# Weight pieces of a fused attention and mixture-of-experts kernel: other staging tiles, deeper staging, a third kind of conversion buffer

## The chip, the core and the metric

The kernel runs on one core of one Trainium2 chip. The core's engines are TensorE (PE in the rows, PEld its weight loads), VectorE (DVE), ScalarE (ACT), GpSimd (POOL) and SyncE (SP), which here does nothing but issue DMAs. The metric is the device time of one execution in microseconds, as a median of runs.

## The reference

Three layers follow one another, for 4 batches, 8 heads, 576 positions and 64 values a head:

```python
scores = scale * np.matmul(q, k.transpose(0, 1, 3, 2))
kth = np.partition(scores, -32, axis=-1)[..., -32:-31]
attn = softmax(np.where(scores >= kth, scores, -1e9))       # the 32 largest of each row
x = (attn @ v), heads side by side: 2304 rows x 512
x = (sigmoid(x @ w_gate) * (x @ w_val)) @ w_out              # 512 -> 1536 -> 512
# then 8 experts, top 2 by noisy logits: relu(x @ w1[e]) @ w2[e], weighted, added
```

The weights w_gate (512 x 1536), w_val (512 x 1536) and w_out (1536 x 512) are read by the kernel as 64-bit words and turned into pairs of 16-bit floats, a high part and the rest, on the chip.

## The kernel before

**Order of the work.** All operations are written down with an engine, an assumed duration, a priority (a lower number goes first), the operations they depend on, and the buffers that they take, each by a tag with a capacity (CAPS, line 174). A planner then goes through assumed time and, on each engine, lets the ready operation of lowest priority number go whose buffers are free. So the order of instructions on each engine is fixed when the kernel is built; on the chip each engine works through its own list, waiting on semaphores where an operand or a buffer isn't ready. Operations that take the same tag on the same engine go in the order in which they were written down.

**Attention** goes in units: one pair of heads (hp, 0 to 3) and one block of 128 query rows, a tile for each head (the last 64 rows of a batch make smaller units). For each, PE makes scores, ACT copies them out (line 355), DVE finds the top values of eight stretches and of these (lines 364 to 373), POOL and ACT prepare the ranking (390, 399, 405), DVE finds the 32nd value and masks the exponents (412, 427), PE transposes them (456, 476) and multiplies by the values (497). The exponents lie in buffers of tag e (4), the ranked copies in y (4). A unit has the priority 10 i, where i counts the tiles before it: 0, 20, 40 and so on. The keys and queries of a head pair of batch 0 are loaded through two st buffers (line 215) with priorities −10, −5, 5 and 15 for the four pairs; the values of the batch (line 259) with −5.

**Gate, value and output layer.** Four units of one row block make a chunk of 128 rows; the first two row blocks of batch 0 are chunks 0 and 1, the next two together are chunk 2 with 256 rows and eight units. A chunk takes a buffer xch (2 of them) when its first unit is opened, ahead of that unit's transposes, and holds it until its last gate and value product. For a chunk, PE goes through 12 hidden blocks of 128 columns (line 537; ACT's tanh, line 544, stands at each), needing weight tile WA[f // 2] for block f, then through the output weights WO (line 576). This work has the unit's priority plus 1000, so it fills what attention leaves of PE.

**The weights.** There are 36 pieces of 512 KB: 24 of w_gate and w_val, four for each of six tiles WA[0] to WA[5] (`wa_ops`), and 12 of w_out, four for each of three tiles WO[0] to WO[2] (`wo_ops`). Their priorities are 0, 4, ..., 20 for WA and 24, 28, 32 for WO. One piece is made by `weight_piece` (lines 265 to 291): SP loads it into an st buffer (274); ACT turns its low words into integers in place (282); DVE puts the bits of the high words into a conversion buffer, two instructions (280, 281); POOL adds the low part (285), after which the st buffer is free; ACT writes the high 16-bit part (286); the rest is made either by DVE (288, one piece in four) or by ACT and POOL (290, 291), after which the conversion buffer is free. The conversion buffers are of tag x2 (2 of them) for two pieces in three and of tag y for the third. There are three st buffers, and the loads of keys, queries and weights take them in the order written down: the four head pairs of batch 0, then the pieces.

The tiles WA and WO come from one pool of nine buffers (`wpool`), which the experts' weights use again later. The tag x2 also serves the layer's result (585) and the first fill of a table (929). Small inputs of the router are loaded by `load_small` (940 to 943), ten DMAs with priority 26.

Of the kernel before, what the change touches and what calls it, by code (L numbers as in the profile page):

```python
# [11 lines left out]
FT = mybir.dt.float32  # L12
FH = mybir.dt.float16
BF = mybir.dt.bfloat16
I32 = mybir.dt.int32
U32 = mybir.dt.uint32
AF = mybir.ActivationFunctionType
# [3 lines left out]
B, H, S, D = 4, 8, 576, 64  # L21
N, DM, F1 = B * S, H * D, 1536
# [104 lines left out]
def attention_moe_kernel(ctx: ExitStack, tc: tile.TileContext, qT, kT, v, w_gate, w_val, w_out,  # L127
# [38 lines left out]
    for b in range(B):  # L166
# [5 lines left out]
    nst = const.tile([128, N // 128, E], FT, name="nst")  # L172

    CAPS = dict(st=3, w=0, tb=4, khl=5, v=5, sS=6, sg=2, m=5, y=4, e=4, pt=2, xch=2, xrem=1, th=2, g=10, x2=2,
                ps=1, tp=3, mm=3, px=3)

    def layers(fast):
        outer = ExitStack()
# [83 lines left out]

        npiece = [0]

        def weight_piece(src, k, f, hi, lo, scale, prio):
            tag = ("x2", "y", "x2")[npiece[0] % 3]
            npiece[0] += 1
            hs, hw = plan.tile("st"), plan.tile(tag)
            t = Unit()

            def load():
                st = stage.tile([128, 2 * S], FT, name="st", bufs=CAPS["st"]).bitcast(I32)[:, :1024]
                t.st = st.rearrange("p (k f c) -> p k f c", k=k, c=2)
                nc.sync.dma_start(t.st.rearrange("p k f c -> p k (f c)"), src.rearrange("(k p) f -> p k f", p=128))
            a = op("SP", 2.6, prio, load, alloc=[hs], lat=3.0)

            def bits():
                t.y = tile_of(tag, [128, SW if tag == "y" else DM], FT)[:, :512].rearrange("p (k f) -> p k f", k=k)
                t.i = t.y.bitcast(I32)
                V.tensor_scalar(t.i, t.st[:, :, :, 1], 3, 0x3FFFFFFF, op0=OP.logical_shift_left, op1=OP.bitwise_and)  # L280
                V.scalar_tensor_tensor(t.i, t.st[:, :, :, 1], -0x40000000, t.i, op0=OP.bitwise_and, op1=OP.bitwise_or)
            r = op("ACT", 0.53, prio, lambda: A.activation(t.st[:, :, :, 0], t.st.bitcast(U32)[:, :, :, 0], AF.Copy,
                                                           scale=2.0 ** -29), [a], use=[hs])
            b = op("DVE", 1.1, prio, bits, [a], alloc=[hw], use=[hs])
            b = op("POOL", 1.2, prio, lambda: G.tensor_tensor(t.i, t.i, t.st[:, :, :, 0], op=OP.add), [r, b], use=[hs, hw])
            c = op("ACT", 0.55, prio, lambda: A.activation(hi(), t.y, AF.Copy, scale=scale), [b], use=[hw])
            if npiece[0] % LOD[0] < LOD[1]:
                return op("DVE", 0.65, prio, lambda: V.scalar_tensor_tensor(lo(), t.y, scale, hi(), op0=OP.mult, op1=OP.subtract),
                          [c], use=[hw])
            d = op("ACT", 0.55, prio, lambda: A.activation(t.y, t.y, AF.Copy, scale=scale), [c], use=[hw])  # L290
            return op("POOL", 1.2, prio, lambda: G.tensor_tensor(lo(), t.y, hi(), op=OP.subtract), [d], use=[hw])  # L291
# [3 lines left out]
        def wa_ops(g, prio):  # L295
# [9 lines left out]
                        sc, prio))  # L305
            WA.append(w)

        def wo_ops(j, prio):
            w = Unit()
            w.h = plan.tile("w")  # L310
            w.t = wpool.tile([128, 4096], FH, name="w").rearrange("p (c k f) -> p c k f", c=2, k=4)
            w.done = [weight_piece(w_out[(4 * j + i) * 128:(4 * j + i + 1) * 128], 1, 512,
                                   lambda i=i: w.t[:, 0, i:i + 1], lambda i=i: w.t[:, 1, i:i + 1], SO, prio)
                      for i in range(4)]
            WO.append(w)


        ranks, scores = [], []
# [623 lines left out]
            for a, src in ((0, wg), (1, wn)):  # L942
                nc.sync.dma_start(wr[:, :, 8 * a:8 * a + 8], src.rearrange("(k p) e -> p k e", p=128))
        if fast:
            op("SP", 5.0, 26, load_small)

        def init_out(prio):
            q, hz = Unit(), plan.tile("x2")
# [109 lines left out]
```

## Time and profile before

| | us |
|---|---|
| median of 3 runs | 1373.16 |
| lowest, highest | 1369.38, 1375.27 |
| the profiled execution | 1367.3 |
| its span, first to last instruction | 1365.5 |
| PE, DVE, ACT, POOL busy in it | 1212.1, 897.1, 814.6, 724.6 |
| mean granted clock of PE | 0.952 |

The profile is of one execution. It gives each instruction of each engine with its start and end, the line of the kernel, and what ended the idle time before it. "Busy" is the union of an engine's instructions, waits on semaphores left out. The granted clock is a share of 2.4 GHz; it has two levels, 1.2 and 2.4 GHz, and a figure between is a mixture over time.

### The profile page before, as it was taken

What the parts mean: (1) busy time and instruction counts of PE and PEld (TensorE: products, weight loads), DVE (VectorE), ACT (ScalarE), POOL (GpSimd) and SP (SyncE); (2) the same over time, 40 slices, a digit from 0 to 9 for tenths busy, and PEclk for the clock granted to TensorE, in tenths of its full rate; (3) what the DMA queues carried; (4) which work ended last, traced back from release to release, by engine and by line L of the source; (5) the groups of instructions that cost most, each with busy time, mean ns of one, the idle gap of its engine ahead of it and who ended that gap; (6) DMA issues with size and microseconds to landing.
All of it is one profiled execution on the core that took longest, in us unless ns stands there. A gap on an engine that the chain in (4) does not pass through costs nothing. (4 is left out here: it accounts for less than half of the span.)

```text
span 1365.5 us, 29938 instructions
## 1 busy us (share of the span) xinstructions
PE 1212.1 (89%) x10829; PEld 899.2 (66%) x10830; DVE 897.1 (66%) x3656; ACT 814.6 (60%) x1818; POOL 724.6 (53%) x985
## 2 busy tenths in 40 slices
PE   2447479699999999999999999899999999999997
PEld 1226356487686868776877778776766666666674
DVE  5998998888999789988778772463233524334221
ACT  4767678777887778777757754562243424424221
POOL 2889998788677586776566562333221222212221
PEclk9667699799999999999999999999999999999999
DMA  8434331362004300051000021264234545443321
GB/s 190 126 107 126 99 124 52 96 174 106 17 14 102 112 2 17 13 132 43 17 2 17 9 94 48 86 208 80 50 94 120 135 81 163 103 107 90 53 45 21
DMA packets 63376, 111.82 MB, mean 82 GB/s; under 512 B 14449, under 2 KB 23793, under 8 KB 63218
## 3 DMA queue, kind: packets, MB, share of 16 engines
q1 hardware_dynamic: 53106, 89.84, 22.3%
q0 software_dynamic: 10112, 19.97, 8.1%
q8 instruction: 87, 1.43, 0.5%
q14 instruction: 71, 0.58, 0.1%
HBM read 79.58 MB, written 20.63 MB: 73 GB/s over the span
## 5 line engine op out<-in xcount | busy, mean ns | idle before, releaser
L537 PEld LDWEIGHTS <-w 128*128 128x128 f16 x3456 | 277.3, 100 | 45.1 <-issue 18.0
L537 PE MATMUL mm<-xch,w 128*128 128x256 f16 (+1 forms) x2880 | 284.1, 256 | 15.0 <-ACT xch L507 5.7
L405 POOL TENSOR_TENSOR y<-sS,sg 128x576 f32<-128x576 f32 x144 | 196.9, 1367 | 9.1
L808 PE MATMUL mm<-xch,w 128*128 128x256 f16 (+1 forms) x2016 | 193.0, 256 | 0.0
L808 PEld LDWEIGHTS <-w 128*128 128x128 f16 x2016 | 170.8, 98 | 23.9
L816 DVE SCALAR_TENSOR_TENSOR g<-mm,g 128x256 f16<-128x256 f32 (+1 forms) x192 | 72.6, 380 | 163.4 <-ACT g L813 162.4
L364 DVE MAX8 cand<-sS 128x8 f32<-128x72 f32 x1152 | 166.7, 217 | 16.4 <-ACT sS L355 16.2
L576 PE MATMUL mm<-w,g 128*128 128x512 f16 x648 | 156.2, 385 | 4.4 <-POOL w L291 2.2
L834 PEld LDWEIGHTS <-g 128*128 128x128 f16 x960 | 93.3, 98 | 98.8
L779 POOL DMA_INDIRECT v<-xd,ids x40 | 42.1, 1052 | 207.6 <-DVE ws L769 192.2
L813 ACT ACTIVATE g<-mm 128x256 f16<-128x256 f32 (+1 forms) x192 | 66.8, 348 | 140.4 <-PE mm L808 134.5
L427 DVE SCALAR_TENSOR_TENSOR e<-sS,good,e 128x576 f32<-128x576 f32 x144 | 139.3, 987 | 1.8 <-ACT e L382 0.7
L554 POOL TENSOR_TENSOR g<-th,g 128x128 f16<-128x128 f32 (+1 forms) x144 | 98.3, 688 | 71.8 <-ACT g L551 70.6
L347 PE MATMUL ps<-khl,qs 128*128 128x288 f16 x512 | 94.6, 313 | 44.9 <-ACT sS L355 26.6
L399 ACT ACTIVATE sg<-sS,m 128x576 bf16<-128x576 f32 x144 | 110.5, 769 | 33.5 <-POOL m L390 33.0
L846 POOL DMA_INDIRECT out<-e,ids x40 | 63.8, 1594 | 123.2 <-ACT e L843 84.8
L412 DVE MAX8 good<-y 128x8 f32<-128x584 f32 x144 | 109.9, 763 | 20.0 <-POOL y L405 15.4
L497 PE MATMUL tp<-pt,v 128*64 128x128 f32 (+3 forms) x1600 | 116.7, 284 | 7.1 <-ACT pt L463 2.8
L834 PE MATMUL tp<-w,g 128*128 128x512 f16 x504 | 114.8, 379 | 0.0
L497 PEld LDWEIGHTS tp<-pt,v 128*64 128x64 f32 (+1 forms) x1600 | 84.6, 142 | 41.0 <-issue 21.1
L456 PE MATMUL tp<-ident,e 128*128 128x128 f32 x576 | 90.0, 291 | 24.4 <-DVE e L427 23.0
L576 PEld LDWEIGHTS <-g 128*128 128x128 f16 x648 | 63.2, 99 | 69.3 <-issue 9.4
(163 smaller groups left out, 2139.3 us busy)
## 6 DMA issues: line engine op xcount, KB each, us to landing
st<-w SPq DMA_DIRECT2D x64, 512.0 KB
khl<-st SPq DMA_DIRECT2D x48, 144.0 KB
st<-w_gate SPq DMA_DIRECT2D x12, 512.0 KB
st<-w_val SPq DMA_DIRECT2D x12, 512.0 KB
st<-w_out SPq DMA_DIRECT2D x12, 512.0 KB
st<-k_t SPq DMA_DIRECT2D x20, 288.0 KB
st<-q_t SPq DMA_DIRECT2D x20, 288.0 KB
xd<-x SPq DMA_DIRECT2D x18, 256.0 KB
```

Of the source, the lines that this page charges most:

```text
L347: P.matmul(o, kqr.qs[:, t, u.q0:u.q0 + 128], kqr.khl[:, c, t, ks], start=c == 0, stop=c == 1)
L364: V.max(T[t].cand[:, 8 * c:8 * c + 8], T[t].s[:, 72 * c:72 * c + 72])
L399: A.activation(T[t].sg, T[t].s, AF.Sign, scale=-CUT[0], bias=T[t].m[:, 25:26], accum_out=T[t].m[:, 26:27])
L405: G.tensor_tensor(T[t].y[:, :S], T[t].s, T[t].sg, op=OP.mult)
L412: V.max(good[:, TILES - 1 - u.i - t:TILES + 7 - u.i - t], T[t].y)
L427: return lambda: V.scalar_tensor_tensor(T[t].e, T[t].s, good[:, TILES + 6 - u.i - t:TILES + 7 - u.i - t], T[t].e, op0=OP.is_ge, op1=OP.mul ...
L497: P.matmul(u.po[64 * s:64 * s + 64, :], VB[u.b, kb][1][:k, (2 * u.hp + s) * D:(2 * u.hp + s + 1) * D], rhs, start=kb == 0, stop=kb == NK - 1)
L537: P.matmul(r.ps[:, a, :], wt.t[:, a, c, kb, fo:fo + 128], ch.x[x][:, kb, :], start=i == 0, stop=i == 11)
L554: G.tensor_tensor(r.g[:, 1], r.th, r.g[:, 0], op=OP.subtract)
L576: P.matmul(r.ps, g[:, c, 128 * t:128 * t + 128], WO[f // 4].t[:, d, f % 4, :], start=f == 0 and i == 0, stop=f == 11 and i == 2)
L808: P.matmul(r.ps, W[kb].w[c][:, 0, f * 128:f * 128 + 128], q.x[x][:, kb, :], start=i == 0, stop=i == 11)
L834: P.matmul(r.ps, gs[f].g[:, c, 128 * t:128 * t + 128], W[4 + f // 2].w[d][:, f % 2, :], start=f == 0 and i == 0, stop=f == 7 and i == 2)
```

## The change

The first 12 gate and value pieces are loaded into halves of the three WO tiles, six slots with a tag of their own each (ws0 to ws5); of the other 12, nine go into the same slots and three into st. The WO tiles are taken from the pool before the WA tiles. For that each WO tile keeps a list of the POOL additions that read from it (`staged`), and the first write of an output piece into the tile, ACT's high part, depends on all of them (`clear`). Output pieces stay in st. The conversion buffers of the pieces are now in turn of tags x2, y and e. The small router inputs get priority 60. The work on a piece is the same.

```diff
--- before.py
+++ after.py
@@ -172,7 +172,7 @@
     nst = const.tile([128, N // 128, E], FT, name="nst")
 
     CAPS = dict(st=3, w=0, tb=4, khl=5, v=5, sS=6, sg=2, m=5, y=4, e=4, pt=2, xch=2, xrem=1, th=2, g=10, x2=2,
-                ps=1, tp=3, mm=3, px=3)
+                ps=1, tp=3, mm=3, px=3, **{f"ws{i}": 1 for i in range(6)})
 
     def layers(fast):
         outer = ExitStack()
@@ -262,20 +262,26 @@
 
         npiece = [0]
 
-        def weight_piece(src, k, f, hi, lo, scale, prio):
-            tag = ("x2", "y", "x2")[npiece[0] % 3]
+        def weight_piece(src, k, f, hi, lo, scale, prio, clear=[]):
+            tag = ("x2", "y", "e")[npiece[0] % 3]
+            i = npiece[0]
+            slot = i % 6 if i < 12 else (i - 12) % 9 if i < 24 and (i - 12) % 9 < 6 else -1
             npiece[0] += 1
-            hs, hw = plan.tile("st"), plan.tile(tag)
+            hs, hw = plan.tile(f"ws{slot}" if slot >= 0 else "st"), plan.tile(tag)
             t = Unit()
 
             def load():
-                st = stage.tile([128, 2 * S], FT, name="st", bufs=CAPS["st"]).bitcast(I32)[:, :1024]
+                if slot >= 0:
+
+                    st = WO[slot // 2].raw[:, 2048 * (slot % 2):2048 * (slot % 2) + 2048].bitcast(I32)
+                else:
+                    st = stage.tile([128, 2 * S], FT, name="st", bufs=CAPS["st"]).bitcast(I32)[:, :1024]
                 t.st = st.rearrange("p (k f c) -> p k f c", k=k, c=2)
                 nc.sync.dma_start(t.st.rearrange("p k f c -> p k (f c)"), src.rearrange("(k p) f -> p k f", p=128))
             a = op("SP", 2.6, prio, load, alloc=[hs], lat=3.0)
 
             def bits():
-                t.y = tile_of(tag, [128, SW if tag == "y" else DM], FT)[:, :512].rearrange("p (k f) -> p k f", k=k)
+                t.y = tile_of(tag, [128, dict(y=SW, e=S, x2=DM)[tag]], FT)[:, :512].rearrange("p (k f) -> p k f", k=k)
                 t.i = t.y.bitcast(I32)
                 V.tensor_scalar(t.i, t.st[:, :, :, 1], 3, 0x3FFFFFFF, op0=OP.logical_shift_left, op1=OP.bitwise_and)
                 V.scalar_tensor_tensor(t.i, t.st[:, :, :, 1], -0x40000000, t.i, op0=OP.bitwise_and, op1=OP.bitwise_or)
@@ -283,7 +289,9 @@
                                                            scale=2.0 ** -29), [a], use=[hs])
             b = op("DVE", 1.1, prio, bits, [a], alloc=[hw], use=[hs])
             b = op("POOL", 1.2, prio, lambda: G.tensor_tensor(t.i, t.i, t.st[:, :, :, 0], op=OP.add), [r, b], use=[hs, hw])
-            c = op("ACT", 0.55, prio, lambda: A.activation(hi(), t.y, AF.Copy, scale=scale), [b], use=[hw])
+            if slot >= 0:
+                WO[slot // 2].staged.append(b)
+            c = op("ACT", 0.55, prio, lambda: A.activation(hi(), t.y, AF.Copy, scale=scale), [b] + clear, use=[hw])
             if npiece[0] % LOD[0] < LOD[1]:
                 return op("DVE", 0.65, prio, lambda: V.scalar_tensor_tensor(lo(), t.y, scale, hi(), op0=OP.mult, op1=OP.subtract),
                           [c], use=[hw])
@@ -305,14 +313,18 @@
                         sc, prio))
             WA.append(w)
 
+        for j in range(3):
+            w = Unit()
+            w.h, w.staged = plan.tile("w"), []
+            w.raw = wpool.tile([128, 4096], FH, name="w")
+            w.t = w.raw.rearrange("p (c k f) -> p c k f", c=2, k=4)
+            WO.append(w)
+
         def wo_ops(j, prio):
-            w = Unit()
-            w.h = plan.tile("w")
-            w.t = wpool.tile([128, 4096], FH, name="w").rearrange("p (c k f) -> p c k f", c=2, k=4)
+            w = WO[j]
             w.done = [weight_piece(w_out[(4 * j + i) * 128:(4 * j + i + 1) * 128], 1, 512,
-                                   lambda i=i: w.t[:, 0, i:i + 1], lambda i=i: w.t[:, 1, i:i + 1], SO, prio)
+                                   lambda i=i: w.t[:, 0, i:i + 1], lambda i=i: w.t[:, 1, i:i + 1], SO, prio, w.staged)
                       for i in range(4)]
-            WO.append(w)
 
 
         ranks, scores = [], []
@@ -942,7 +954,7 @@
             for a, src in ((0, wg), (1, wn)):
                 nc.sync.dma_start(wr[:, :, 8 * a:8 * a + 8], src.rearrange("(k p) e -> p k e", p=128))
         if fast:
-            op("SP", 5.0, 26, load_small)
+            op("SP", 5.0, 60, load_small)
 
         def init_out(prio):
             q, hz = Unit(), plan.tile("x2")
```

## Rows read from the trace of the kernel before

**Rows 1.** Page, busy tenths in 40 slices of 34.1 us:

```profile
PE   2447479699999999999999999899999999999997
PEclk9667699799999999999999999999999999999999
```

**Rows 2.** Stages: from:to, us, busy PE PEld DVE ACT POOL, PEclk, DMA share, GB/s:

```profile
0.00:40.00 40.00, 11.68 (x55) 7.00 (x57) 23.79 (x86) 21.97 (x35) 12.99 (x38) 1.00 0.78 184
40.00:200.00 160.00, 89.94 (x790) 65.31 (x790) 153.36 (x496) 117.88 (x252) 145.66 (x154) 0.73 0.37 115
200.00:280.00 80.00, 64.21 (x611) 47.47 (x612) 67.20 (x323) 61.12 (x137) 63.61 (x90) 0.85 0.32 82
280.00:1366.00 1086.00, 1046.30 (x9377) 779.43 (x9374) 652.70 (x2753) 613.66 (x1396) 502.30 (x706) 0.99 0.28 73
```

**Rows 3.** Timeline, SP's queue: start us, us, queue, line, DMA, tensors:

```profile
0.83 1.42 SPq L215 DMA_DIRECT2D st<-k_t  x2
12.88 0.59 SPq L940 DMA_DIRECT2D nst<-noise  x1
31.26 4.52 SPq L274 DMA_DIRECT2D st<-w_gate  x2
146.08 49.24 SPq L274 DMA_DIRECT2D st<-w_out  x12
```

**Rows 4.** Timeline, ACT, 37 to 39 us:

```profile
37.77 0.67 ACT L282 ACTIVATE st<-st 128x512 int32<-128x512 uint32 x1
```

**Rows 5.** Sums by stage, the first 40 us in two:

```profile
0.00:20.00 20.00, 2.26 (x8) 1.00 (x9) 7.51 (x21) 7.19 (x9) 2.54 (x25) 1.00 0.91 209
20.00:40.00 20.00, 9.42 (x47) 6.00 (x48) 16.29 (x66) 14.78 (x26) 10.45 (x13) 1.00 0.64 158
```

**Rows 6.** Page, DMA issues by line: count and size of each:

```profile
st<-k_t SPq DMA_DIRECT2D x20, 288.0 KB
```

**Rows 7.** Groups, 0 to 300 us: conversion steps; busy us, mean ns, idle:

```profile
L280 DVE TENSOR_SCALAR x<-st 128x512 int32<-128x512 int32 x24 | 18.1, 754 | 0.0
L280 DVE TENSOR_SCALAR y<-st 128x512 int32<-128x512 int32 x12 | 11.3, 941 | 0.0
L281 DVE SCALAR_TENSOR_TENSOR x<-st,x 128x512 int32<-128x512 int32 x24 | 23.2, 965 | 0.8
L281 DVE SCALAR_TENSOR_TENSOR y<-st,y 128x512 int32<-128x512 int32 x12 | 14.2, 1184 | 0.4
L285 POOL TENSOR_TENSOR x<-x,st 128x512 int32<-128x512 int32 x24 | 34.2, 1427 | 5.4 <-DVE x L281 1.4 <-ACT px L483 1.2 <-DVE m L442 1.1
L285 POOL TENSOR_TENSOR y<-y,st 128x512 int32<-128x512 int32 x12 | 16.2, 1348 | 1.4 <-issue 0.7 <-POOL w L291 0.7
L291 POOL TENSOR_TENSOR w<-x,w 128x512 f16<-128x512 f32 x18 | 23.4, 1304 | 1.5 <-ACT x L290 1.4
L291 POOL TENSOR_TENSOR w<-y,w 128x512 f16<-128x512 f32 x9 | 11.9, 1321 | 0.0
```

**Rows 8.** Waits of PE, 40 to 200 us: us in total, times, longest:

```profile
PE ps L347 <- ACT sS L355: 20.2, 9, 4.3
PE tp L456 <- DVE e L427: 16.7, 8, 6.7
PE tp L474 <- POOL px L446: 16.4, 7, 5.1
PE mm L576 <- POOL w L291: 2.2, 2, 2.0
```

**Rows 9.** Timeline, ACT: chunk 0's tenth, twelfth, chunk 2's first hidden block:

```profile
135.84 0.28 ACT L544 ACTIVATE th<-mm 128x128 f32<-128x128 f32 x1 [0.44 <-PE mm L537]
...
174.32 0.27 ACT L544 ACTIVATE th<-mm 128x128 f32<-128x128 f32 x1
...
273.22 0.38 ACT L544 ACTIVATE th<-mm 128x256 f32<-128x256 f32 x1
```

**Rows 10.** One line's instructions: count, ns min/median/max, first and last start:

```profile
L280 DVE TENSOR_SCALAR x<-st x24: 399/429/1500, 39.1 to 202.7; 128x512 int32<-128x512 int32 x24
```

## The prediction

> **What bounds the kernel now.** I read the slices of the whole span first, then the sums by stage, then the queue that issues the loads, then the groups of the conversion. In the slices [rows 1] PE is at 0.9 or more from the ninth slice on and far below that before it; the granted clock of the first eight slices is lower too. The sums by stage [rows 2] say the same in microseconds. From 280 us to the end PE is idle for 1086.0 − 1046.3 = 39.7 us, 4%. Before 280 us it is idle for 28.3 + 70.1 + 15.8 = 114.2 us, and its busy time there runs at a mean clock of 0.73 (40 to 200 us) and 0.85 (200 to 280 us), a mixture of the two levels 1.2 and 2.4 GHz, which costs about 89.9 × 0.27 + 64.2 × 0.15 = 33.9 us more. So the start loses some 148 us of PE, and the rest of the kernel is PE-bound. The change touches only the start.
>
> In the start the bound is elsewhere. From 40 to 200 us DVE is busy 153.4 of 160 us and POOL 145.7 of 160 [rows 2]. PE's own waits in that stretch [rows 8] are on attention: on the copies out of the score bank (20.2 us), on the masked exponents from DVE (16.7 us), on POOL's spread of the reciprocals (16.4 us). For converted weights it waits 2.2 us in the largest such row. PE is short of work because two vector engines carry attention and 36 weight pieces at once. After that, from 200 to 280 us, no weight is left to load, but PE still lacks 15.8 us and DVE is idle for 12.8 us: this is a tail, read below.
>
> **The change part by part.**
>
> **Earlier loads.** The piece loads stood in line for the three st buffers behind the eight key and query loads of batch 0. The queue of SP [rows 3] shows it: first key load at 0.83 us, first weight load at 31.26 us, the last group (twelve output pieces) from 146.08 us. The first converting instruction ran at 37.77 us [rows 4]. With a tag of their own the first pieces can go at their priority 0, which is behind the loads of head pairs 0 and 1 and of the values, and ahead of pairs 2 and 3. Ahead of the first piece there are then 4 key and query tiles of 2 × 288 KB [rows 6] and 1.18 MB of values (576 × 512 × 4 bytes), 3.5 MB, which at the 209 GB/s of the first 20 us [rows 5] take 17 us, and the piece's 512 KB (128 × 1024 × 4 bytes) 2.5 us more. So it lands at about 20 us, 18 us sooner. That isn't worth 18 us, since the vector engines weren't waiting all of it. From 20 to 40 us DVE had 3.7 us idle and POOL 9.6 [rows 5]; from 0 to 20 us the 12.5 idle us of DVE stay, as nothing more has landed. I take 3.7 us, from the fuller engine; bounds 0 and 9.6.
>
> **Deeper staging.** 21 of the 24 gate and value pieces lie in the unfilled output tiles. No step of a piece goes away: in the groups [rows 7] the two bit steps on DVE are 18.1 + 11.3 + 23.2 + 14.2 = 66.8 us, the two POOL steps 34.2 + 16.2 + 23.4 + 11.9 = 85.7 us, and all of it stays. What the depth changes is the order: pieces have lower priority numbers than all units but the first, so DVE and POOL will take more weights and less attention early, and the reverse later. Between 40 and 200 us DVE has only 6.6 us idle [rows 2], so reordering by itself gains there from 0 to 6.6 us; I take 0.
>
> Why the order can still matter is the tail. Chunk 0 (128 rows) finishes its tenth hidden block at 135.84 us and its twelfth only at 174.32 us [rows 9], for the last weight tile comes late. Until then it holds one of the two xch buffers, chunk 1 holds the other, and chunk 2 can't be opened; no unit of it can pass its transposes. Chunk 2's first hidden block stands at 273.22 us [rows 9], and from then PE is full. With the gate and value weights done some tens of us sooner, the buffer comes free as soon as chunk 0 is there, and units flow without the gap. What is late next is the vector work itself: chunk 2's eight units. So of the 12.8 us of DVE idle in 200 to 280 us [rows 2] I expect 10 back; bounds 0 (the idle time belongs to chains inside a unit, which stay) and 12.8. A microsecond taken out of DVE ahead of chunk 2 moves the moment from which PE is full by one.
>
> **Three kinds of conversion buffers.** The x2 tag carried 24 pieces, now 12; the e tag carries 12 that it shares with the exponents. The steps cost the same in any buffer. A piece holds its buffer for its steps, by [rows 7] 1.9 us on DVE and 2.4 on POOL, with ACT's between them, and exponents of attention may wait for it; x2 is freer for the evictions and the table's fill. I count 0; no row shows exponents waiting for e, so the bounds are one such hold, −4 and +4 us.
>
> **The added wait.** The first ACT step of an output piece now waits for the POOL additions of all pieces that were staged in its tile. Behind it on ACT stand exponents and evictions. By priority these additions come before the output pieces' own on POOL, which work in order, so the wait is met when its turn comes; if not, it is one addition per tile, 3 × 1.4 us [rows 7] = 4 us. I count 0.
>
> **The small loads.** They took SP from 12.88 us [rows 3], ten DMAs between key loads, and now go behind the weights, at a moment when the weight loads wait for a slot. They feed the first router, which comes after chunk 0's last hidden block at 174.32 us [rows 9]. 0, bounds −2 and +2 us.
>
> **The sum.** 3.7 + 0 + 10 + 0 + 0 = 13.7, or 14 us, against the profiled execution: 1367.3 − 14 = 1353 us (its span is 1365.5). That execution is 5.9 us under the median of the three runs, 1373.2 us, so the prediction on the median's scale is **1359 us**.
>
> **A rule that speaks against it.** DVE's shift of a piece takes 399 ns at best and up to 1500 ns [rows 10], with the same shape each time; something takes turns with it. The Trainium skill (SBUF — State Buffer, "Who interferes with whom") says that a DVE instruction with two SBUF inputs, or one in a two-port mode, and a GpSimd instruction share one port pair as an exclusive lock, the second fully blocked until the first ends. The spread agrees. By the rule a denser stretch of conversions buys nothing, since the pair is taken already: that is the first rival.
>
> **The rivals.**
> - **The two vector engines are one resource.** In a piece the two-input DVE step takes (23.2 + 14.2) / 36 = 1.04 us and POOL's steps 85.7 / 36 = 2.38 us [rows 7]; if these exclude each other, a piece needs 3.4 us, 36 of them 123 us, and POOL's own 145.7 us in 160 [rows 2] leave no room. Then the idle time between 20 and 40 us can't be filled well, the tail keeps its chains, and the gain is at most the 3.7 us: **1370 us**, no change that can be told. For it: the near-full rows of both engines at the same time. Against it: the tail after 200 us isn't full on either (67.2 and 63.6 of 80 us).
> - **The queue of SP blocks attention (slower).** The key and query loads of head pairs 2 and 3 now stand behind 8 and 16 pieces on SP, an in-order queue, and a piece's load waits there until a slot's POOL addition is done. DVE's splitting steps for these pairs stand at fixed places in its own order, chosen with assumed times. If the loads are late there, DVE stops with the rest behind it. Four loads, each late by the time from a load to its use, 37.77 − 31.26 = 6.5 us [rows 3, 4], make 26 us; less the 14 of the forecast it is 12 us slower: **1385 us**. It decides when DVE's idle time from 20 to 100 us grows by more than 14 us. For it: 209 GB/s at the start [rows 5] shows a loaded memory path already. Against it: slots turn over with the same conversions that fill DVE, so there is mostly something to do.
> - **All of it comes back.** The upper bounds together, 9.6 + 6.6 + 12.8 = 29 us, and some 6 us of the clock loss in the tail (9.6 us by [rows 2]), make 35 us: **1338 us**. This is the far end of the forecast's own case.
>
> **How the numbers follow.** The forecast's case, from 7 to 35 us gained, has 0.60; no change to be told 0.22; the blocked queue 0.18. What a measurement of this kernel can tell from no change is about 0.5%, 7 us. The range that should hold the time 8 times in 10 runs from the far end of the first case, 1338, to just short of the slower rival, 1382; that leaves out most of the slower rival and little else. Faster by over 0.5% 0.60, within 0.5% 0.22, slower 0.18.
>
> **What would show it.** Right: the first converting instruction near 20 us, not 37.8; the last shift well before 202.7 us [rows 10]; no gap between the tenth and the twelfth hidden block of chunk 0; chunk 2's first hidden block near 259 us; the sums after 280 us unchanged. For the first rival: conversions early, but chunk 2 still near 270 us with DVE and POOL full till then. For the second: waits of DVE or ACT on key and query DMAs between 20 and 100 us, and chunk 0's tenth hidden block after 136 us [rows 9]. The forecast is wrong altogether if the difference arises after 280 us, where the change puts nothing, or if PE, with its own order fixed beforehand, comes to wait for weights that the vector engines deliver later than that order assumed.

## The result, and the profile after

| | before | changed |
|---|---|---|
| median, us | 1372.8 | 1384.4 |
| lowest, highest | 1367.0, 1379.4 | 1379.4, 1386.3 |
| the profiled execution | 1367.3 | 1384.4 |
| its span | 1365.5 | 1382.6 |

The changed kernel is slower: ratio 1.0085, 95% interval 1.0067 to 1.0103, 11.6 us between the medians. The two profiled executions lie 17.1 us apart, since that of the kernel before is 5.5 us below its median; what follows explains the profiled pair, and then asks how much of it is the change's. Lines move down by up to 12: 347 is 359, 456 is 468, 537 is 549, 544 is 556.

The page of the changed kernel, the slices of PE and its granted clock, to hold against [rows 1]:

```profile
PE   1223889799899999999999999899999999999997
PEclk9855899799999999999999999999999999999998
```

PE is emptier for four slices (some 137 us), then fuller or as full for four. The sums by stage, with the columns of [rows 2] (PE, PEld, DVE, ACT, POOL, granted clock, DMA share, GB/s):

```profile
0.00:40.00 40.00, 4.52 (x16) 1.99 (x17) 27.26 (x81) 20.98 (x34) 19.37 (x40) 1.00 0.84 236
40.00:200.00 160.00, 83.34 (x733) 61.12 (x734) 149.96 (x440) 116.32 (x238) 141.52 (x148) 0.72 0.40 120
200.00:280.00 80.00, 67.94 (x681) 51.98 (x680) 71.54 (x354) 59.68 (x146) 59.25 (x89) 0.87 0.23 53
280.00:1383.00 1103.00, 1054.80 (x9410) 782.71 (x9405) 655.93 (x2784) 616.99 (x1403) 496.32 (x710) 0.99 0.28 72
```

PE's idle time up to 280 us is 35.5 + 76.7 + 12.1 = 124.2 us, 10.0 more than before; after 280 us it is 48.2, 8.5 more. PE's busy time is 1.5 us less. That is the 17 us. The split at 120 us shows how the first part came about, first the kernel before, then the changed one:

```profile
0.00:120.00 120.00, 55.19 (x426) 39.63 (x428) 100.52 (x341) 80.61 (x157) 81.61 (x113) 0.79 0.50 135
120.00:280.00 160.00, 110.64 (x1029) 80.14 (x1029) 143.84 (x562) 120.37 (x267) 140.64 (x168) 0.82 0.35 101
```

```profile
0.00:120.00 120.00, 29.57 (x145) 17.75 (x146) 106.21 (x252) 75.60 (x133) 89.16 (x100) 0.75 0.61 178
120.00:280.00 160.00, 126.23 (x1281) 97.34 (x1283) 142.55 (x622) 121.39 (x283) 130.99 (x177) 0.84 0.26 72
```

Up to 120 us PE is idle for 90.4 us in place of 64.8, though DVE and POOL are busier than before (106 and 89 us); from 120 to 280 us it wins back 15.6 of these 25.6 us and no more. The timeline of ACT in the changed kernel has the marks of [rows 4] and [rows 9]: the first converting instruction, then the tanh of chunk 0's first, tenth and twelfth hidden block and of chunk 2's first:

```profile
19.77 0.68 ACT L288 ACTIVATE w<-w 128x512 int32<-128x512 uint32 x1 [0.69 <-DMA w<-w_gate]
...
148.33 0.28 ACT L556 ACTIVATE th<-mm 128x128 f32<-128x128 f32 x1 [0.36 <-PE mm L549]
...
171.00 0.27 ACT L556 ACTIVATE th<-mm 128x128 f32<-128x128 f32 x1
...
179.06 0.28 ACT L556 ACTIVATE th<-mm 128x128 f32<-128x128 f32 x1 [1.55 <-PE mm L549]
...
278.46 0.39 ACT L556 ACTIVATE th<-mm 128x256 f32<-128x256 f32 x1 [1.90 <-PE mm L549]
```

The weights came 18 us sooner, the gap inside chunk 0 is gone (8 us between the tenth and the twelfth block, 38 before), and still the chunk itself came later: its tenth block at 171 us and not at 136, its first at 148 us and not at 105, as this row of the kernel before has it. Chunk 2 starts at 278 us and not at 273.

```profile
104.57 0.28 ACT L544 ACTIVATE th<-mm 128x128 f32<-128x128 f32 x1 [0.29 <-PE mm L537]
```

The queue of SP and the longest waits of PE up to 120 us in the changed kernel (columns: us in total, times, longest) say why chunk 0 was late:

```profile
11.16 1.11 SPq L280 DMA_DIRECT2D w<-w_gate  x2
...
25.48 1.25 SPq L215 DMA_DIRECT2D st<-k_t  x2
...
58.44 1.26 SPq L215 DMA_DIRECT2D st<-k_t  x2
```

```profile
PE ps L359 <- DVE qs L223: 26.1, 3, 11.3
PE tp L486 <- POOL px L458: 22.4, 3, 8.2
PE tp L468 <- POOL m L402: 17.8, 1, 17.8
```

PE waits on attention's vector steps, as in [rows 8]. The keys of pairs 2 and 3 are loaded at 25 and 58 us, behind pieces, and what DVE does meanwhile is weights. Its shifts (line 280, now 286; one for each piece) and its rankings (line 412, now 424; two for each unit) up to 120 us show it, first in the kernel before, then in the changed one (DVE's busy us and count, then granted clock, DMA share, GB/s):

```profile
0.00:120.00 120.00, 13.63 (x17) 0.79 0.50 135
0.00:120.00 120.00, 9.92 (x13) 0.79 0.50 135
```

```profile
0.00:120.00 120.00, 22.15 (x27) 0.75 0.61 178
0.00:120.00 120.00, 5.24 (x7) 0.75 0.61 178
```

DVE has converted ten pieces more and ranked six tiles fewer. Chunk 0 needs eight rankings, four units of two tiles, and hasn't got them by then.

### The profile page after: what moved, and what is told of

It reads as the page before. It is cut to its first block, busy times and chain, and to the rows that moved or that the text cites. A ratio compares the mean times of both kernels' runs of the same rounds, so it can differ in the third digit from the quotient of the medians.

```text
span 1382.6 us, 29937 instructions
## 1 busy us (share of the span) xinstructions
PE 1210.6 (88%) x10829; PEld 897.8 (65%) x10830; DVE 904.7 (65%) x3656; ACT 814.0 (59%) x1818; POOL 716.5 (52%) x985
## 5 line engine op out<-in xcount | busy, mean ns | idle before, releaser
L828 DVE SCALAR_TENSOR_TENSOR g<-mm,g 128x256 f16<-128x256 f32 (+1 forms) x192 | 72.5, 380 | 167.3 <-ACT g L825 166.7
L846 PEld LDWEIGHTS <-g 128*128 128x128 f16 x960 | 93.5, 98 | 99.7 <-issue 0.8
L588 PE MATMUL mm<-w,g 128*128 128x512 f16 x648 | 151.8, 379 | 0.0
L439 DVE SCALAR_TENSOR_TENSOR e<-sS,good,e 128x576 f32<-128x576 f32 x144 | 144.4, 1028 | 3.2 <-ACT e L394 2.4
L566 POOL TENSOR_TENSOR g<-th,g 128x128 f16<-128x128 f32 (+1 forms) x144 | 89.5, 626 | 74.8 <-ACT g L563 74.1
L424 DVE MAX8 good<-y 128x8 f32<-128x584 f32 x144 | 109.8, 763 | 17.8 <-POOL y L417 13.3
L394 ACT ACTIVATE e<-sS,m 128x576 f32<-128x576 f32 x144 | 107.1, 768 | 2.2 <-POOL w L299 1.6
```

The costliest lines, as they stand in the source:

```text
L394: A.activation(T[t].e, T[t].s, AF.Exp, bias=T[t].m[:, CM:CM + 1], scale=SC)
L424: V.max(good[:, TILES - 1 - u.i - t:TILES + 7 - u.i - t], T[t].y)
L439: return lambda: V.scalar_tensor_tensor(T[t].e, T[t].s, good[:, TILES + 6 - u.i - t:TILES + 7 - u.i - t], T[t].e, op0=OP.is_ge, op1=OP.mul ...
L588: P.matmul(r.ps, g[:, c, 128 * t:128 * t + 128], WO[f // 4].t[:, d, f % 4, :], start=f == 0 and i == 0, stop=f == 11 and i == 2)
L846: P.matmul(r.ps, gs[f].g[:, c, 128 * t:128 * t + 128], W[4 + f // 2].w[d][:, f % 2, :], start=f == 0 and i == 0, stop=f == 7 and i == 2)
```

## The experiments

Three theories were held against each other. **SP order**: the key and query loads behind the pieces make units 2 and 3 late. **Weights first**: the pieces' low priority numbers make DVE, POOL and ACT take weights ahead of units, whatever SP does. **Contention**: the same steps take longer where DVE's two-input instructions and POOL's run densely side by side. A fourth came from the first results, **the order's scatter**: any new order of the same work moves the time.

### Parts of the change undone or made alone

Keys and queries of batch 0 ahead of the pieces on SP alone:

```diff
-                lk = op("SP", 1.6, prio, load("k", kT), alloc=[hs[0], r.h], lat=3.0)
-                lq = op("SP", 1.6, prio, load("q", qT), [lk], alloc=[hs[1]], lat=3.0)
+                lk = op("SP", 1.6, min(prio, -5), load("k", kT), alloc=[hs[0], r.h], lat=3.0)
+                lq = op("SP", 1.6, min(prio, -5), load("q", qT), [lk], alloc=[hs[1]], lat=3.0)
```

> The changed kernel with one edit: the key and query loads of all four head pairs of batch 0 have priority -5 or lower, so that on SP they go ahead of the weight pieces; all else as changed (staging, buffers, and the priorities on the other engines). Before 1373 us, changed 1384 us; PE idle in the first 120 us 65 and 90 us. If the loads of pairs 2 and 3 behind 8 and 16 pieces make units 2 and 3 late and so cost the time (theory 'SP order'): PE idle up to 120 us falls to 65 to 75 us, the time to 1368 to 1376 us. If the weights take the vector engines ahead of the units whatever SP does (theory 'weights first'): PE idle stays at 85 us or more, the time within 4 us of 1384. If denser conversion makes DVE's two-input steps longer (theory 'contention'): no change, 1380 to 1388 us.

Measured: 1379.6 us against 1371.3 of the kernel before on the same chip, ratio 1.0057 (1.0035 to 1.0078). The row of its first 120 us:

```profile
0.00:120.00 120.00, 30.91 (x145) 18.05 (x146) 105.43 (x275) 76.48 (x134) 91.50 (x100) 1.00 0.62 182
```

PE is busy for 30.9 us there, idle for 89.1: next to nothing won back (89.1 against 90.4), with the last of these loads issued at 24 us, behind three pieces in place of 16. SP's order isn't what empties PE. The time, 4.4 us under the changed kernel's median where "weights first" allowed 4, lies within the spread of orders measured below.

The pieces' priorities spread over the first six units, on every engine:

```diff
-            wa_ops(g, PW + 4 * g)
+            wa_ops(g, PW + 15 * g)
-            wo_ops(j, PW + 24 + 4 * j)
+            wo_ops(j, PW + 90 + 15 * j)
```

> The changed kernel with one edit: the pieces' priorities are 0, 15, ..., 75 for the gate and value tiles and 90, 105, 120 for the output tiles, in place of 0, 4, ..., 20 and 24, 28, 32, so that they interleave with the first six units (priorities 0, 20, ..., 100) on every engine. Theory 'weights first': units of chunk 0 come as early as before the change, PE idle up to 120 us falls to 65 to 75 us, and with the early loads kept the time is 1362 to 1374 us. Theory 'SP order': the same, since the loads of pairs 2 and 3 come ahead of the pieces with higher numbers too; the run with the loads alone tells the two apart. Theory 'contention': conversions spread out again, the DVE time of the steps falls by the 6 us that it rose, 1376 to 1382 us.

Measured: 1371.7 against 1371.3 us, ratio 1.000 (0.998 to 1.002). Its first 120 us:

```profile
0.00:120.00 120.00, 52.62 (x416) 37.77 (x418) 101.58 (x320) 82.25 (x159) 87.53 (x114) 0.82 0.57 166
```

PE is idle for 67.4 us, as before the change, and the loss is gone, with the staging, the buffers and the early loads all as changed. This is "weights first" by its own numbers. "SP order" expected the same of this run, but the run before this one rules it out; "contention" expected 1376 to 1382 us, and shorter bit steps, which did come (72.5 to 65.8 us). DVE's shifts and rankings up to 120 us, 20 and 12 here, are near those of the kernel before again:

```profile
0.00:120.00 120.00, 16.57 (x20) 0.82 0.57 166
0.00:120.00 120.00, 9.17 (x12) 0.82 0.57 166
```

The conversion buffers as before, the staging as changed (and, next, the reverse):

```diff
-            tag = ("x2", "y", "e")[npiece[0] % 3]
+            tag = ("x2", "y", "x2")[npiece[0] % 3]
```

> The changed kernel with the conversion buffers as before (tags x2, y, x2), the staging as changed. If the e buffers, shared with the exponents, hold attention up: the time falls towards 1373 us. By 'SP order', 'weights first' and 'contention' the e buffers do nothing of themselves: within 5 us of 1384 us, perhaps less late as two x2 buffers slow the conversion down and let attention in (1376 to 1384 us).

Measured: 1390.3 us, ratio 1.0137 (1.0099 to 1.0176), 6 us above the changed kernel and not below it. The e buffers aren't what holds attention up.

```diff
-            tag = ("x2", "y", "x2")[npiece[0] % 3]
+            tag = ("x2", "y", "e")[npiece[0] % 3]
-                t.y = tile_of(tag, [128, SW if tag == "y" else DM], FT)
+                t.y = tile_of(tag, [128, dict(y=SW, e=S, x2=DM)[tag]], FT)
```

> The kernel before with one edit: the conversion buffers in turn of tags x2, y and e, the staging as before in three st buffers. If the buffers were what held conversion back, and faster conversion is what costs: conversions end earlier than 208 us, units come later, 1376 to 1384 us. If staging is what counts: within 4 us of 1373 us, with the last conversion within 10 us of 208 us.

Measured: 1379.0 us, ratio 1.0054 (1.0034 to 1.0073). The time is in the range of the first theory in that expectation, but its mechanism isn't there: the last step of a conversion started at 215 us, not earlier than 208, and PE's idle time up to 280 us is 112.9 us against 114.2. A kernel that does the same up to 280 us and is 7 us slower asked for the scatter of orders to be measured.

### Less work for POOL

In both kernels, 27 low parts made as copies:

```diff
-            d = op("ACT", 0.55, prio, lambda: A.activation(t.y, t.y, AF.Copy, scale=scale), [c], use=[hw])
-            return op("POOL", 1.2, prio, lambda: G.tensor_tensor(lo(), t.y, hi(), op=OP.subtract), [d], use=[hw])
+            return op("ACT", 0.55, prio, lambda: A.activation(lo(), t.y, AF.Copy, scale=scale), [c], use=[hw])
```

> The kernel before, with part of the computation left out: in 27 of 36 weight pieces the low 16-bit part isn't the rest after the high part but a second copy of it, by one ACT instruction in place of ACT's scaling and POOL's subtraction. That takes 27 x 1.3 = 35 us off POOL, and shortens how long a conversion buffer is held; DVE's work stays. If DVE and POOL together bound the start (theory 'vector engines'): PE idle up to 280 us falls from 114 to 85 to 105 us, the time from 1372 to 1345 to 1365 us. If DVE alone bounds it: PE idle falls by less than 5 us, the time stays within 5 us.

> The changed kernel with the same part left out as in the run of the kernel before (27 low parts are copies, 35 us less of POOL). Theory 'weights first': the weights still go ahead of the units but take less, so PE idle up to 120 us falls from 90 to 75 to 85 us, and the kernel stays 4 to 12 us behind the kernel before with the same part left out. Theory 'contention' (the loss is that POOL's steps lengthen DVE's two-input steps while they come densely): the distance to the kernel before with the same part left out closes to within 3 us.

Measured: 1359.5 and 1378.1 us, ratios to the kernel before 0.9932 (0.9915 to 0.9948) and 1.0068 (1.0051 to 1.0084). The low parts are left out, and with them ACT's scaling and POOL's subtraction; POOL's additions stay. Their stages up to 280 us, first the kernel before with less, then the changed one:

```profile
0.00:120.00 120.00, 57.18 (x478) 42.54 (x479) 102.28 (x354) 86.88 (x177) 75.34 (x110) 0.79 0.56 153
120.00:280.00 160.00, 120.71 (x1145) 90.19 (x1144) 146.58 (x608) 124.66 (x283) 125.45 (x167) 0.86 0.37 104
```

```profile
0.00:120.00 120.00, 38.93 (x192) 24.41 (x194) 104.44 (x296) 87.62 (x161) 76.29 (x97) 0.91 0.64 191
120.00:280.00 160.00, 127.76 (x1349) 99.36 (x1348) 144.28 (x646) 116.90 (x280) 111.47 (x168) 0.89 0.25 68
```

Taking 35 us of POOL's work away takes 10 us off the kernel before: PE's idle time up to 280 us goes from 114.2 to 62.8 + 39.3 = 102.1 us. That is within what was expected if POOL and DVE together bound the start, which the prediction read out of the trace; it bears out POOL's part, in one order, and DVE's work was not varied. The distance of the changed kernel to it did not close, it grew to 18.7 us, with 81.1 us of idle PE up to 120 us against 62.8. "Weights first" had expected 75 to 85 us of idle time, which came, and a distance of 4 to 12 us, which didn't; two single orders, by the spread below, are a poor measure of a distance. The plainer evidence is the time of the two bit steps, the changed kernel with less (shift, then two-input step, DVE's busy us up to 280 us):

```profile
0.00:280.00 280.00, 25.91 (x36) 0.90 0.42 121
...
0.00:280.00 280.00, 36.00 (x36) 0.90 0.42 121
```

That is 61.9 us, less than the 66.8 us before the change, so the steps are no longer lengthened, and PE's idle time up to 120 us is still 18 us above that of the kernel before with less. Contention with POOL isn't what empties PE; what it adds to these steps is read below, under the tail.

### Other orders of the same work

The planner's assumed duration of ACT's high part, 0.55 us, is changed by 0.01 or 0.02 us. No instruction is added or taken away; the lists of all engines change in many places.

```diff
-            c = op("ACT", 0.55, prio, lambda: A.activation(hi(), t.y, AF.Copy, scale=scale), [b], use=[hw])
+            c = op("ACT", 0.56, prio, lambda: A.activation(hi(), t.y, AF.Copy, scale=scale), [b], use=[hw])
```

The kernel before, with 0.56, 0.54 and 0.53:

> The kernel before with one assumed duration of the planner changed by nothing that matters: ACT's high part of a piece counts 0.56 in place of 0.55 us. The work is the same, the planner's order differs in many places. It measures what a new order alone does. Theory 'the change's loss and the differences of 5 to 8 us between the first four runs are the scatter of orders': the time lies 4 to 12 us from 1372, to either side. Theory 'they have causes of their own': within 3 us.

> The kernel before with the same assumed duration at 0.54 in place of 0.55 us: another order of the same work. If a new order alone costs and the order of the kernel before is at the good end of its neighbours: 1375 to 1382 us, with PE idle up to 280 us at 110 to 116 us as in its other neighbours, and the difference after 280 us. If the first neighbour (1380 us) was an outlier: 1369 to 1374 us.

> The kernel before with the assumed duration of ACT's high part at 0.53 in place of 0.55 us. If the design before has a mean of about 1375 us with a scatter of orders of some 5 us to either side: 1370 to 1380 us, PE idle up to 280 us 108 to 116 us.

The changed kernel, with 0.56, 0.54 and 0.57 (in all three the dependencies read `[b] + clear`):

> The changed kernel with the same assumed duration at 0.56 in place of 0.55 us. Scatter of orders: 4 to 12 us from 1384, to either side. Causes of their own: within 3 us of 1384, with PE idle up to 120 us at 85 to 95 us again.

> The changed kernel with 0.54 in place of 0.55 us. Theory 'weights first': PE idle up to 280 us lies at 122 to 132 us, as in all kernels of the changed priorities so far (124, 129, 130, 129), 10 us or more above every neighbour of the kernel before (111 to 114); the time 1380 to 1392 us. If the change's loss is only a new order's: PE idle up to 280 us somewhere between 110 and 130, the time 1372 to 1392 us.

> The changed kernel with 0.57 in place of 0.55 us. Theory 'weights first': PE idle up to 280 us 122 to 132 us once more and 1379 to 1389 us. If the loss is of the order only: PE idle up to 280 us below 120, the time anywhere from 1370 us.

The changed kernel with the spread priorities, with 0.56 and 0.54:

> The changed kernel with the pieces' priorities spread (0, 15, ..., 75 and 90, 105, 120) and the assumed duration at 0.56 us: a neighbour of the run with spread priorities (1372 us, PE idle up to 280 us 111). Theory 'weights first': PE idle up to 280 us again at 108 to 116 us, the time 1368 to 1380 us as the order after 280 us falls out. If that run was a lucky order: PE idle up to 280 us 120 us or more and 1380 us or more.

> The changed kernel with spread priorities and 0.54 in place of 0.55 us. If the staging with spread priorities gains by its design: PE idle up to 280 us 108 to 113 us, the time 1360 to 1372 us. If 1362 us was a lucky order: 1372 to 1382 us.

Spread priorities and the two edits of the key and query loads together, with 0.55, 0.56 and 0.53:

> The changed kernel with spread priorities, and the key and query loads of batch 0 ahead of all pieces on SP as well. If any of the loss came from SP's queue: PE idle up to 120 us falls from 65 to 67 us by 3 us or more, and the time lies below the mean of the runs with spread priorities. If SP's queue plays no part: PE idle up to 280 us within 4 us of 110, the time 1360 to 1374 us.

> The changed kernel with spread priorities and key and query loads first, and ACT's high part at 0.56 in place of 0.55 us. If the combination gains by its design: 1358 to 1368 us, PE idle up to 280 us 106 to 110 us. If 1361 us was a lucky order: 1368 to 1380 us.

> The same with 0.53 us. Design: 1358 to 1368 us, PE idle up to 280 us 106 to 110 us. Lucky order: 1368 to 1380 us.

And the spread priorities in the kernel before, its staging as it was:

> The kernel before, staging and buffers as they were, with the pieces' priorities spread to 0, 15, ..., 75 and 90, 105, 120: weights still later than in the kernel before. Theory 'weights first is what costs': units come earlier still, PE idle up to 120 us falls below 62 us; the last piece ends after 215 us, and as the last gate tiles are then late for chunk 0, the gain stops: PE idle up to 280 us 106 to 116 us, the time 1365 to 1380 us. If earlier weights help in themselves (what the prediction held): slower, PE idle up to 280 us over 118 us and 1380 us or more.

All orders together; ratios are to the kernel before on the same chip, idle is PE's in the profiled execution, in us:

| design | median, us | ratio (95% interval) | idle to 120 us | idle to 280 us |
|---|---|---|---|---|
| before, own order | 1369 to 1373 | 1 | 64.8 | 114.2 |
| before, 0.56 | 1380.2 | 1.0074 (1.0055 to 1.0093) | 66.5 | 113.4 |
| before, 0.54 | 1373.8 | 1.0022 (1.0004 to 1.0039) | 63.0 | 108.9 |
| before, 0.53 | 1378.9 | 1.0055 (1.0032 to 1.0078) | 63.5 | 108.6 |
| changed, own order | 1384.4 | 1.0085 (1.0067 to 1.0103) | 90.4 | 124.2 |
| changed, 0.56 | 1387.3 | 1.0129 (1.0098 to 1.0159) | 89.6 | 128.5 |
| changed, 0.54 | 1379.4 | 1.0065 (1.0039 to 1.0091) | 89.2 | 124.4 |
| changed, 0.57 | 1374.7 | 1.0029 (1.0009 to 1.0048) | 90.3 | 121.4 |
| changed, spread | 1371.7 | 1.0000 (0.9979 to 1.0021) | 67.4 | 111.4 |
| changed, spread, 0.56 | 1361.6 | 0.9928 (0.9903 to 0.9952) | 64.6 | 108.8 |
| changed, spread, 0.54 | 1377.2 | 1.0057 (1.0040 to 1.0074) | 67.5 | 110.4 |
| changed, spread, keys first | 1360.8 | 0.9934 (0.9908 to 0.9960) | 67.1 | 108.1 |
| the same, 0.56 | 1373.2 | 1.0024 (1.0004 to 1.0044) | 66.5 | 105.1 |
| the same, 0.53 | 1360.7 | 0.9929 (0.9902 to 0.9956) | 66.4 | 104.1 |
| before, spread | 1379.1 | 1.0062 (1.0039 to 1.0086) | 63.9 | 115.1 |

Two things are to be read here. First, an order alone moves the time by 11 to 16 us within one design (1369 to 1380, 1375 to 1387, 1362 to 1377, 1361 to 1373 us). Second, the design shows through it in the idle time: up to 120 us, 63 to 68 us in every row of the kernel before and every one with spread priorities, 89 to 90 in the four of the changed one with its own priorities. DVE's counts of shifts and rankings up to 120 us go with it: 17 to 20 and 12 or 13 in the four orders of the kernel before, 27 and 6 or 7 in the four of the changed one, 20 or 21 and 12 in the six with spread priorities.

The last row of the table has 17 and 12. It had been expected to bring PE's idle time up to 120 us below 62 us, and that stayed at 63.9: with three st buffers the pieces run no further ahead with one set of numbers than with the other. It took the deep staging to give the low numbers their effect, and the staging alone did it: the changed kernel with the old conversion buffers has 26 and 6, the kernel before with the new ones 18 and 12.

The mean ratios are 1.0038 for the four orders of the kernel before, 1.0077 for the four of the changed one, 0.9979 for the six of the changed one with spread priorities.

So the changed design is 0.39%, some 5 us, behind the design before, with a standard deviation of 0.3 and 0.4% between single orders: four orders each don't settle that difference. By the same means, the other half of the 11.6 us is that the kernel before stands at the good end of its own orders. What the runs do show is the work of the priorities: with the same staging, buffers and early loads, the six orders with spread ones are on the mean 0.98%, some 13 us, ahead of the four changed ones. Three of the six have the key and query loads first as well; the three without have a mean of 0.9995, which is 11 us ahead, but with a standard deviation of 0.65% between them. So the idle time, where the two sets don't overlap, is the firm part, and the size in time is rough. The key and query loads first bring chunk 2's first block from 270 to 265 us on the mean of three orders each; whether the time follows (means 1364.9 and 1370.1 us) stays open. The fastest two, 1360.7 and 1360.8 us, beat both kernels; that is the design and a good order together, and the third order of the same design, 1373.2 us, shows the share of the order.

## Why the prediction was wrong, point by point

**What bounds the start: right as far as it was tried.** DVE and POOL together; the run with less work for POOL shows POOL's part, DVE's rests on its full rows.

**Earlier loads: right in mechanism, and in size as DVE's idle time.** Forecast: first conversion near 20 us, 3.7 us of DVE's idle time between 20 and 40 us back. Measured: 19.77 us, the last shift at 166.9 us in place of 202.7, and this row of the changed kernel against [rows 5]:

```profile
20.00:40.00 20.00, 2.13 (x8) 0.86 (x6) 19.39 (x60) 12.87 (x24) 16.84 (x15) 1.00 0.76 223
```

DVE's idle time there is 0.6 us, 3.1 less. But PE's busy time in the same row fell from 9.4 to 2.1 us, and no run shows that the 3.1 us shortened the kernel.

**Deeper staging: the step that failed.** The prediction saw that DVE and POOL would take more weights and less attention early, and priced the new order at 0 with bounds 0 and 6.6 us, a gain or nothing. (Its reason, numbers below those of all units but the first, holds for the pieces with 0 to 16; the sixth gate and value tile has 20 like the second unit, and the output pieces, 24 to 32, come behind that unit.) It counted only the vector engines' idle time; with these bounds the order between weights and units could not cost anything. But of the two kinds of vector work only units feed PE at once; weights feed it only when a chunk is there to use them. By 120 us DVE had done 27 shifts and 7 rankings in place of 17 and 13, PE had been idle for 25.6 us more, and chunk 0's first hidden block came at 148 us in place of 105. The price of the new order against spread priorities is some 13 us by the means above, 11 us by the three orders that differ in nothing else, on the other side of a bound that was put at zero.

**The tail: half right.** The gap within chunk 0 closed, as forecast. The 10 us of DVE time weren't won: DVE's idle time from 200 to 280 us went from 12.8 to 8.5 us. Over the first 280 us it went from 35.6 to 31.2 us, and DVE's busy time rose by the same 4.4 us for the same 36 pieces and 36 rankings. The sums by stage of the changed kernel, over 280 us and for one line each (DVE's busy us, then granted clock, DMA share, GB/s), show where it lies: the two-input bit step (line 281, now 287) and the shift (280, now 286), 37.4 and 29.4 us before by [rows 7], are 5.7 us longer together:

```profile
0.00:280.00 280.00, 41.57 (x36) 0.80 0.41 117
...
0.00:280.00 280.00, 30.89 (x36) 0.80 0.41 117
```

That isn't this pair's alone: the two steps take 66.8, 69.2, 66.9 and 68.6 us in the four orders of the kernel before, 72.5, 73.0, 71.7 and 74.5 in the four of the changed one, and 65.8, 66.5 and 65.2 with spread priorities alone. The prediction kept them at 66.8 us; where the conversions stand densely they are some 5 us longer, and in this pair that took up what was gained. What the 5 us cost in time no run shows by itself. The forecast of 259 us for chunk 2's first block failed. In the four orders of the kernel before it stood at 273, 278, 279 and 270 us, in the four of the changed one at 278, 278, 277 and 271: no difference. With the spread priorities it stood at 269, 270 and 270 us, with the keys first as well at 264, 263 and 267 us: there a part of the forecast gain exists. As time, the whole forecast of 14 us, 1%, is in no mean: 0.9995 for the three orders with spread priorities alone, against 1.0038 for the kernel before.

**Buffers, the added wait, the small loads: no cost told apart.** Each was put at 0. The e buffers cost nothing that stands out of the scatter (1390 us without them, 1384 with); up to 280 us ACT waited 30.2 us for POOL's additions ahead of its high parts, 21.1 before; the wait for an own and for a staged addition can't be told apart there, and nothing was tried to do so. The small loads weren't undone alone either; the runs with spread priorities keep both, and their PE is no emptier than before.

**After 280 us: wrong.** The prediction said that the sums there stay. PE's idle time after 280 us rose by 8.5 us, half of the 17 us of the profiled pair, and the prediction had named a difference there as a sign that it was wrong altogether. In the other orders of the kernel before it varies as much: between 280 and 800 us it is 11.9 us in its own order, 17.8, 9.6 and 18.9 in the three others, against 17.8, 19.0, 12.8 and 15.2 in the four of the changed design. So this part is no larger than the order's scatter, which the prediction had no term for, in the sum or in the range.

**The rivals.** The blocked queue gave 1385 us, the nearest number of all, but that is luck. It was to show in DVE's idle time from 20 to 100 us growing by over 14 us, and this fell from 4.6 to 1.5 us; with the keys ahead of the weights PE stays as empty. One of its signs, chunk 0's tenth block after 136 us, came true by the other way. The first rival, two vector engines as one resource, is nearest to what happened up to 280 us: conversions early and chunk 2 no sooner, though DVE and POOL weren't full till then (71.5 and 59.3 of 80 us from 200 us). Its 1370 us left out what the units' delay costs PE. On the Trainium skill's rule (SBUF — State Buffer, "Who interferes with whom"): DVE's shift took from 408 to 2156 ns in the changed kernel for one shape, which agrees with taking turns, but with POOL's 35 us gone the bit steps were shorter than before the change and PE's idle time up to 120 us still 18 us longer, so turns at the port aren't what separates the kernels there.

## What to carry to other kernels

Where two kinds of work share a full engine, ask which of them feeds the engine that sets the end, and when; a busy engine isn't a reason to price their order at zero. Bound an edit of a planned order from both sides by orders of the same work: here a hundredth of a microsecond in an assumed duration moved the time by up to 13 us (1374.7 and 1387.3), as much as the change under study. And judge a design by several orders, since one order can hide it: the staging that came out 12 us slower is, on the mean of six orders with priorities that let attention through, some 8 us ahead of the four of the kernel before (0.9979 and 1.0038). Three of the six have the key and query loads first as well, and so few orders don't settle a difference of that size.

## What the runs showed of the hardware

The granted clock's column can read 1.00 where PE isn't at its full clock. In one order of the changed kernel (0.57 us) the sums from 60 to 140 us give 1.00, but in the same stretch a score matmul of 288 columns took 438 ns on the mean, and 286 ns after 280 us. The row of the stage, and the groups of line 359 in it and from 280 to 600 us (busy us, mean ns, idle):

```profile
60.00:140.00 80.00, 30.37 (x147) 18.77 (x148) 77.47 (x203) 54.76 (x103) 70.14 (x62) 1.00 0.45 137
...
L359 PE MATMUL ps<-khl,qs 128*128 128x288 f16 x40 | 11.3, 438 | 26.3 <-ACT sS L367 19.0 <-DVE qs L223 7.3
...
L359 PE MATMUL ps<-khl,qs 128*128 128x288 f16 x236 | 38.6, 286 | 1.8 <-ACT sS L367 1.8
```

The changed kernel's own order has the same matmul at 419 ns in this stretch, and there the column reads 0.52, mostly the low level:

```profile
60.00:140.00 80.00, 26.01 (x129) 16.00 (x129) 77.97 (x204) 55.15 (x105) 69.42 (x62) 0.52 0.46 135
...
L359 PE MATMUL ps<-khl,qs 128*128 128x288 f16 x32 | 8.6, 419 | 20.5 <-ACT sS L367 11.2 <-DVE qs L223 9.2
```

So 438 ns goes with the low level, and the 1.00 beside it is not to be believed; PE was busy for 30 of those 80 us. The Trainium skill (TensorE: Matmul & The Clock Gate, "What's actually happening") says that the low state is the default and activity lifts it; the durations agree, the column doesn't. So matmul durations are the safer witness, and the prediction's 34 us of clock loss, taken from the column, is a rough figure. It leaves out the first 40 us, where [rows 2] have 1.00 and the score matmul of the kernel before took 436 ns on the mean:

```profile
L347 PE MATMUL ps<-khl,qs 128*128 128x288 f16 x24 | 6.8, 436 | 21.4 <-DVE qs L223 17.3 <-ACT sS L355 4.0
```

Nor is idle PE time by itself the loss. The four orders of the changed design have 13 us more of it up to 280 us than those of the kernel before (124.6 and 111.3 on the mean), but 10 us less busy time over the whole span (1208.6 and 1218.3). The score matmul's mean over the whole span is 306 to 308 ns in them and 309 to 313 in the others, which fits work that moved to where it runs at the high level; no run tested that by itself.
